# A linear-attention and MLP-mixer kernel: fp32 loads on the hardware queue, work moved to GpSimd, one activation table set, and two PSUM banks for three

## The chip, the cores and the metric

The kernel runs on one core of a Trainium2 chip. The metric is device time in microseconds of one execution. A core has TensorE (PE), VectorE (DVE), ScalarE (ACT), GpSimd (POOL) and SyncE (SP), each of which works through its own queue in order, and 16 DMA engines that all of them feed.

## The reference

Four batches, eight heads, 768 steps, head size 48. First a gated linear attention with a state per head, then a mixer: a token MLP (768 to 256 to 768) and a channel MLP (384 to 1536 to 384), each added to its input.

```python
f = 1.0 / (1.0 + np.exp(-f_logit))
for t in range(S):
    state = f[:, :, t, :, None] * state + np.einsum('bhd,bhe->bhde', k[:, :, t], v[:, :, t])
    y[:, :, t] = np.einsum('bhd,bhde->bhe', q[:, :, t], state)
# x = y with the heads side by side: (4, 768, 384)
h = np.maximum(xt @ w_tok1, 0.0) @ w_tok2          # xt = x transposed
u = x + h.transpose(0, 2, 1)
out = u + np.maximum(u @ w_ch1, 0.0) @ w_ch2
```

## The kernel before, in words

A sequence is cut into six chunks of 128 steps. For a whole batch (for batch 0: chunk 0, then the other five together) `prep_gates_slices` makes the logarithm of the gate on ACT, exp then ln, and splits it into two bf16 parts, Lhi (ACT) and Llo (DVE).

For each chunk `attn_front` sums the gates along time on PE into ps_S, and their totals into ps_dg. `attn_chunk` then makes G and Gi (ACT, exp of minus and plus the sum), multiplies q by G and k by Gi (qh and kh, both on DVE, lines 177 and 178), transposes both with eight matmuls against an identity into the two banks ps_AT, copies these as bf16 to qkT (q half on ACT, line 185, k half on DVE, line 186), multiplies k by q per head into the same banks (line 191), masks the result (AmT, two DVE operations, lines 200 and 201), and multiplies it with v into ps_y, to which the carried state adds its part. ACT copies ps_y to x_nat (fp32) and x_bf (bf16). Five DVE operations carry the state on.

`moe_slices` is the mixer of one batch: token matmuls (lines 247 and 254, evicted to h1T, u_nat and u_bf), transposes of u (line 268, to uT), 24 groups of three channel matmuls (line 280, each evicted to zT by ACT, one in three by DVE), and six groups of twelve output matmuls (line 298), added to u on DVE and stored by SP from two buffers out_sb. Its matmuls go round three PSUM banks. The mixer's six slices of one batch are written into the six chunks of the next batch's attention; a scheduler then puts the instructions of each engine in a fixed order, which the engine follows.

Loads: q, k and v are cast from fp32 to bf16 by DMAs that GpSimd issues; f_logit comes in fp32 on SP's queue. For batch 0 they are issued chunk by chunk, for the others in one DMA each. The weights are loaded, also cast, by GpSimd, after the inputs of batches 0 and 1. Batch b + 2 is loaded into the buffers of batch b. [...]

Of the kernel before, what the change touches and what calls it, by code (L numbers as in the profile page):

```python
# [17 lines left out]
def kernel(  # L18
# [24 lines left out]
    def st(shape, dtype, tag):  # L43
        return sb.tile(shape, dtype, tag=tag, name=tag)
# [19 lines left out]
        nc.gpsimd.dma_start(out=w_ch1, in_=moe_w_ch1.rearrange("(kt p) n -> p kt n", p=128))  # L64
        nc.gpsimd.dma_start(out=w_ch2, in_=moe_w_ch2.rearrange("(kt p) n -> p kt n", p=128))

    q_sb = [st([128, H, NCH, D], BF16, f"q_sb{i}") for i in range(2)]
    k_sb = [st([128, H, NCH, D], BF16, f"k_sb{i}") for i in range(2)]
    v_sb = [st([128, H, NCH, D], BF16, f"v_sb{i}") for i in range(2)]
    f_sb = [st([128, H, NCH, D], FP32, f"f_sb{i}") for i in range(2)]  # L70
    Lhi = [st([128, NCH, H, 64], BF16, f"Lhi{i}") for i in range(2)]
    Llo = [st([128, NCH, H, 64], BF16, f"Llo{i}") for i in range(2)]

    def load_batch_inputs(b, c0=0, c1=NCH):
        i = b % 2
        if (c0, c1) == (0, NCH):
            nc.gpsimd.dma_start(out=q_sb[i], in_=q[b].rearrange("h (c t) d -> t h c d", t=C))
            nc.gpsimd.dma_start(out=k_sb[i], in_=k[b].rearrange("h (c t) d -> t h c d", t=C))
            nc.gpsimd.dma_start(out=v_sb[i], in_=v[b].rearrange("h (c t) d -> t h c d", t=C))
            nc.sync.dma_start(out=f_sb[i], in_=f_logit[b].rearrange("h (c t) d -> t h c d", t=C))  # L80
            return
        for c in range(c0, c1):
            nc.sync.dma_start(out=f_sb[i][:, :, c, :],
                              in_=f_logit[b].rearrange("h (c t) d -> t h c d", t=C)[:, :, c, :])
            nc.gpsimd.dma_start(out=q_sb[i][:, :, c, :],
                                in_=q[b].rearrange("h (c t) d -> t h c d", t=C)[:, :, c, :])
            nc.gpsimd.dma_start(out=k_sb[i][:, :, c, :],
                                in_=k[b].rearrange("h (c t) d -> t h c d", t=C)[:, :, c, :])
            nc.gpsimd.dma_start(out=v_sb[i][:, :, c, :],
                                in_=v[b].rearrange("h (c t) d -> t h c d", t=C)[:, :, c, :])  # L90

    G = [st([128, H, 64], BF16, f"G{i}") for i in range(2)]
    Gi = [st([128, H, 64], BF16, f"Gi{i}") for i in range(2)]
# [17 lines left out]
    nc.vector.memset(state_bd, 0.0)  # L111

    ps_S = pt([128, 512], FP32, "ps_S")
    ps_AT = [pt([128, 4, 128], FP32, f"ps_AT{p}") for p in range(2)]
    ps_y = pt([128, H, D], FP32, "ps_y")
    ps_dg = pt([128, HP, 2 * D + 1], FP32, "ps_dg")
# [4 lines left out]
    uT = st([128, 3, S], BF16, "uT")  # L121
    zT = st([128, 12, S], BF16, "zT")
    out_sb = [st([128, DM], FP32, f"out_sb{i}") for i in range(2)]
    ps_moe = [pt([128, 512], FP32, f"ps_moe{i}") for i in range(3)]
    ring = [0]

    def moe_bank():
        ring[0] += 1
        return ps_moe[ring[0] % 3]

    def prep_gates_slices(b, c0=0, c1=NCH):
        ib = b % 2
# [33 lines left out]
    def attn_chunk(b, c, mid=(), front_next=None):  # L166
        i = c % 2
        ib = b % 2
        last = c == NCH - 1

        sview = ps_S.rearrange("t (h dd) -> t h dd", dd=64)[:, :, 0:D]
        nc.scalar.activation(G[i][:, :, 0:D], sview, AF.Exp, bias=0.0, scale=-1.0)
        nc.scalar.activation(Gi[i][:, :, 0:D], sview, AF.Exp, bias=0.0, scale=1.0)
        if not last:
            nc.scalar.activation(glast, ps_dg[:, :, 2 * D], AF.Exp, bias=0.0, scale=-1.0)  # L175

        nc.vector.tensor_tensor(qh[i][:, :, 0:D], q_sb[ib][:, :, c, :], G[i][:, :, 0:D], ALU.mult)
        nc.vector.tensor_tensor(kh[i][:, :, 0:D], k_sb[ib][:, :, c, :], Gi[i][:, :, 0:D], ALU.mult)

        qb, kb = blk(qh[i]), blk(kh[i])  # L180
        for hp in range(HP):
            nc.tensor.matmul(ps_AT[0][:, hp, :], lhsT=qb[:, hp, :], rhs=ident, start=True, stop=True)
        for hp in range(HP):
            nc.tensor.matmul(ps_AT[1][:, hp, :], lhsT=kb[:, hp, :], rhs=ident, start=True, stop=True)
        nc.scalar.copy(qkT[i][:, 0:4, :], ps_AT[0])  # L185
        nc.vector.tensor_copy(qkT[i][:, 4:8, :], ps_AT[1])  # L186

        for h in range(H):
            hp, par = h // 2, h % 2
            rows = slice(par * 64, par * 64 + D)  # L190
            nc.tensor.matmul(ps_AT[par][:, hp, :], lhsT=qkT[i][rows, 4 + hp, :],  # L191
                             rhs=qkT[i][rows, hp, :], start=True, stop=True)

        if front_next is not None:
            front_next()
        for m in mid:
            m()

        tb4 = tri_bf.unsqueeze(1).broadcast_to((128, 4, 128))
        nc.vector.tensor_tensor(AmT[i][:, 0:4, :], ps_AT[0], tb4, ALU.mult)  # L200
        nc.vector.tensor_tensor(AmT[i][:, 4:8, :], ps_AT[1], tb4, ALU.mult)

        for h in range(H):
            nc.tensor.matmul(ps_y[:, h, :], lhsT=AmT[i][:, (h % 2) * 4 + h // 2, :],
                             rhs=v_sb[ib][:, h, c, :],
                             start=(h == 0), stop=(c == 0 and h == H - 1),
                             skip_group_check=True)
        if c > 0:
            for hp in range(HP):
                nc.tensor.matmul(ps_y[:, 2 * hp:2 * hp + 2, :], lhsT=qkT[i][:, hp, :],  # L210
                                 rhs=state_bd[:, hp, :],
                                 start=False, stop=(hp == HP - 1), skip_group_check=True)
        if not last:
            for hp in range(HP):
                nc.tensor.matmul(ps_dg[:, hp, 0:2 * D], lhsT=kb[:, hp, :],
                                 rhs=v_sb[ib][:, 2 * hp:2 * hp + 2, c, :],
                                 start=True, stop=True)

        yflat = ps_y.rearrange("t h e -> t (h e)")
        nc.scalar.activation(x_nat[ib][:, c, :], yflat, AF.Copy, bias=0.0, scale=1.0)  # L220
        nc.scalar.activation(x_bf[ib][:, c, :], yflat, AF.Copy, bias=0.0, scale=1.0)

        if not last:
            nc.vector.tensor_tensor(state[0:D], state[0:D], ps_dg[0:D, :, 0:D], ALU.add)  # L224
            nc.vector.tensor_tensor(state[64:64 + D], state[64:64 + D],  # L225
                                    ps_dg[64:64 + D, :, D:2 * D], ALU.add)
            nc.vector.tensor_tensor(state, state, glast.unsqueeze(2).broadcast_to((128, HP, D)),  # L227
                                    ALU.mult)
            nc.vector.tensor_copy(state_bd[0:D, :, 0:D], state[0:D])
            nc.vector.tensor_copy(state_bd[64:64 + D, :, D:2 * D], state[64:64 + D])  # L230
# [7 lines left out]
    def moe_slices(b):  # L238
# [3 lines left out]

        def s_tok():
            for rt in range(2):
                pm = moe_bank()
                for kt in range(NCH):
                    nc.tensor.matmul(pm[:, 0:DM], lhsT=w_tok1[:, kt, rt * 128:(rt + 1) * 128],  # L247
                                     rhs=x_bf[ib][:, kt, :],
                                     start=(kt == 0), stop=(kt == NCH - 1))
                nc.scalar.activation(h1T[:, rt, :], pm[:, 0:DM], AF.Relu, bias=0.0, scale=1.0)  # L250
            for stt in range(NCH):
                pm = moe_bank()
                for kt in range(2):
                    nc.tensor.matmul(pm[:, 0:DM], lhsT=w_tok2[:, kt, stt * 128:(stt + 1) * 128],
                                     rhs=h1T[:, kt, :], start=(kt == 0), stop=(kt == 1))
                nc.vector.tensor_tensor(u_nat[:, stt, :], x_nat[ib][:, stt, :], pm[:, 0:DM], ALU.add)  # L256
                nc.scalar.activation(u_bf[:, stt, :], u_nat[:, stt, :], AF.Copy,  # L257
                                     bias=0.0, scale=1.0)
            if _DBG:
                nc.sync.dma_start(out=dbg_u[b].rearrange("(c t) n -> t c n", t=C), in_=u_nat)  # L260
                nc.sync.dma_start(out=dbg_h1[b], in_=h1T)
        sl.append(s_tok)

        def s_ut():
            for dmb in range(3):
                pm = moe_bank().bitcast(BF16)
                for stt in range(NCH):
                    nc.tensor.transpose(pm[:, stt * 128:(stt + 1) * 128],
                                        u_bf[:, stt, dmb * 128:(dmb + 1) * 128], ident)
# [5 lines left out]
        def s_ch(cc0, cc1, alt):  # L275
            for cc in range(cc0, cc1):
                for th in range(2):
                    pm = moe_bank()
                    for kt in range(3):
                        nc.tensor.matmul(pm[:, 0:384], lhsT=w_ch1[:, kt, cc * 128:(cc + 1) * 128],  # L280
                                         rhs=uT[:, kt, th * 384:(th + 1) * 384],
# [10 lines left out]
        def s_out():  # L292
            if _DBG:
                nc.sync.dma_start(out=dbg_zT[b], in_=zT)
            for tt in range(NCH):
                pm = moe_bank()
                for kt in range(12):
                    nc.tensor.matmul(pm[:, 0:DM], lhsT=zT[:, kt, tt * 128:(tt + 1) * 128],  # L298
                                     rhs=w_ch2[:, kt, :], start=(kt == 0), stop=(kt == 11))
# [6 lines left out]
    if _DBG:  # L306
# [2 lines left out]
        dbg_h1 = nc.dram_tensor("dbg_h1", (B, 128, 2, DM), BF16, kind="Internal").ap()  # L309
        dbg_uT = nc.dram_tensor("dbg_uT", (B, 128, 3, S), BF16, kind="Internal").ap()  # L310
        dbg_zT = nc.dram_tensor("dbg_zT", (B, 128, 12, S), BF16, kind="Internal").ap()
    load_batch_inputs(0, 0, 2)
    load_batch_inputs(0, 2, NCH)
    load_batch_inputs(1)
    load_weights()
    prev_moe: list = []
    for g in prep_gates_slices(0, 0, 1) + prep_gates_slices(0, 1, NCH):
        g()
    for b in range(B):
        ib = b % 2  # L320
        attn_batch_begin(b)
# [17 lines left out]
            nc.sync.dma_start(out=dbg_x[b].rearrange("(c t) n -> t c n", t=C),  # L339
                              in_=x_nat[b % 2])  # L340
        if b + 2 < B:
            load_batch_inputs(b + 2)
        prev_moe = moe_slices(b)
    for s in prev_moe:
        s()
# [30 lines left out]
```

## Time and profile before

| | us |
|---|---|
| median of 2 runs (242.51 to 243.28) | 242.89 |
| the profiled execution, its own time | 242.51 |
| its span, first to last instruction | 240.4 |

| engine | busy us | share of the span | instructions |
|---|---|---|---|
| PE, matmuls | 183.6 | 76% | 1673 |
| PE, weight loads | 111.5 | 46% | 1688 |
| DVE | 152.1 | 63% | 341 |
| ACT | 137.2 | 57% | 262 |
| POOL | 40.1 | 17% | 39 |

The software queue (GpSimd) moved 10.23 MB in 77168 packets, the hardware queue (SP) 9.44 MB in 14352.

How to read it: busy time is the sum over an engine's instructions. The profile also gives the span in 40 slices of 6 us, each digit the busy share of a slice in tenths. Groups show line, engine, operation and tile, with their count, sum, the mean of one in ns, and what ended the idle time before them. A view of waits says who waited for whom, with the total, the count and the longest. A view of stages gives each engine's busy time between two times, and a timeline gives start and duration of each instruction.

### The profile page before, as it was taken

The numbers are of one execution on the slowest core, as the hardware profiler recorded it, in microseconds if no ns is written. First come the engines' busy times: TensorE is split into PE (matmuls) and PEld (weight loads), VectorE is DVE, ScalarE is ACT, GpSimd is POOL, SyncE is SP. The second block draws the span as 40 slices with busy tenths as digits, with TensorE's granted clock in tenths as the row PEclk, the third lists the DMA queues.
The fourth block names the chain that finished last, engine by engine and source line by source line (L and its number), as shares of the span: only waits on it lengthen the run. The fifth ranks groups of instructions, "written<-read, shape, count | busy, mean of one in ns | idle before, by whom it ended". The sixth has DMA issues, their size and how long they took to land.

```text
span 240.4 us, 4273 instructions
## 1 busy us (share of the span) xinstructions
PE 183.6 (76%) x1673; PEld 111.5 (46%) x1688; DVE 152.1 (63%) x341; ACT 137.2 (57%) x262; POOL 40.1 (17%) x39
## 2 busy tenths in 40 slices
PE   0413376103858999999999999999999999989993
PEld 0201253001535555566565555666556556546661
DVE  4323769300965999995489998637999872444221
ACT  5479999900697765870376777008776710556300
POOL 9823910821302100150300000000000000000000
PEclk9999999999965999999999999999999999999999
DMA  8999999999999900099490000121000002100022
GB/s 113 147 185 151 163 158 137 174 144 198 208 182 137 103 3 0 3 85 174 135 104 0 3 1 3 65 100 35 0 3 0 3 33 102 64 0 0 8 107 85
DMA packets 91539, 19.93 MB, mean 83 GB/s; under 512 B 80896, under 2 KB 91136, under 8 KB 91520
## 3 DMA queue, kind: packets, MB, share of 16 engines
q0 software_dynamic: 77168, 10.23, 78.3%
q1 hardware_dynamic: 14352, 9.44, 18.4%
q8 instruction: 13, 0.21, 0.4%
q14 instruction: 6, 0.05, 0.1%
HBM read 25.17 MB, written 4.72 MB: 124 GB/s over the span
## 4 chain that ended last, share of the span: by engine, by line
PE 34%; DVE 26%; DMA 15%; issue 9%; ACT 8%; POOL 7%; DVEq 0%; POOLq 0%
DMA q_sb_77<-in_q_dram 6%; DMA w_tok_73<-in_moe_w_tok_dram 6%; PE ps_moe_135 L298 5%; PE ps_moe_133 L298 5%; PE ps_moe_134 L298 5%; PE ps_moe_133 L280 3%; DMA out_dram<-out_sb_132 3%; DVE zT L285 3%; PE ps_moe_134 L280 3%; PE ps_moe_135 L280 3%; DVE u_nat L256 2%; DVE qkT_98 L186 2%; DVE AmT_99 L200 2%; DVE uT L270 2%; DVE state L225 2%
## 5 line engine op out<-in xcount | busy, mean ns | idle before, releaser
L298 PEld LDWEIGHTS <-zT 128*128 128x128 bf16 x288 | 27.7, 98 | 18.3
L280 PEld LDWEIGHTS <-w_ch_75 128*128 128x128 bf16 x288 | 26.5, 97 | 19.9 <-issue 4.5
L280 PE MATMUL ps_moe_133<-uT,w_ch_75 128*128 128x384 bf16 x96 | 22.9, 325 | 1.4 <-DVE uT L270 0.5
L280 PE MATMUL ps_moe_135<-uT,w_ch_75 128*128 128x384 bf16 x96 | 22.6, 325 | 0.8 <-DVE zT L285 0.5
L280 PE MATMUL ps_moe_134<-uT,w_ch_75 128*128 128x384 bf16 x96 | 22.2, 325 | 0.5 <-DVE zT L285 0.3
L220 ACT ACTIVATE x_nat_105<-ps_y 128x384 f32<-128x384 f32 x12 | 6.0, 499 | 24.8 <-PE ps_y L210 24.2
L298 PE MATMUL ps_moe_134<-w_ch_76,zT 128*128 128x384 bf16 x96 | 17.3, 326 | 0.0
L200 DVE TENSOR_TENSOR AmT_100<-ps_AT_122,tri_bf 128x512 bf16<-128x512 f32 x12 | 8.3, 688 | 14.2 <-PE ps_AT_123 L191 14.0
L298 PE MATMUL ps_moe_135<-w_ch_76,zT 128*128 128x384 bf16 x96 | 17.1, 326 | 0.0
L298 PE MATMUL ps_moe_133<-w_ch_76,zT 128*128 128x384 bf16 x96 | 17.1, 326 | 0.0
L287 ACT ACTIVATE zT<-ps_moe_134 128x384 bf16<-128x384 f32 x22 | 10.9, 496 | 8.0 <-PE ps_moe_134 L280 7.8
L161 PE MATMUL ps_dg<-ones_bf,Lhi_85 128*128 128x1 bf16 x40 | 3.5, 166 | 13.5 <-ACT Lhi_85 L143 6.7
L287 ACT ACTIVATE zT<-ps_moe_135 128x384 bf16<-128x384 f32 x22 | 11.0, 500 | 4.9 <-PE ps_moe_135 L280 4.8
L220 ACT ACTIVATE x_nat_104<-ps_y 128x384 f32<-128x384 f32 x12 | 5.8, 486 | 13.9 <-PE ps_y L210 13.9
L247 PE MATMUL ps_moe_134<-x_bf_106,w_tok_73 128*128 128x384 bf16 x6 | 2.5, 452 | 14.1 <-DMA w_tok_73<-in_moe_w_tok_dram 12.2
L247 PEld LDWEIGHTS <-w_tok_73 128*128 128x128 bf16 x48 | 4.6, 105 | 17.9 <-DMA w_tok_73<-in_moe_w_tok_dram 12.4
L287 ACT ACTIVATE zT<-ps_moe_133 128x384 bf16<-128x384 f32 x20 | 10.0, 500 | 4.3 <-PE ps_moe_133 L280 4.2
L224 DVE TENSOR_TENSOR state<-state,ps_dg 48x192 f32<-48x192 f32 x20 | 6.8, 342 | 8.5 <-ACT qkT_98 L185 4.9
L257 ACT ACTIVATE u_bf<-u_nat 128x384 bf16<-128x384 f32 x24 | 11.0, 519 | 1.8 <-DVE u_nat L256 1.6
L200 DVE TENSOR_TENSOR AmT_99<-ps_AT_122,tri_bf 128x512 bf16<-128x512 f32 x12 | 8.2, 685 | 6.0 <-PE ps_AT_123 L191 5.7
L175 ACT ACTIVATE glast<-ps_dg 128x4 f32<-128x4 f32 x20 | 3.6, 178 | 14.1 <-DVE state L227 12.7
L191 PE MATMUL ps_AT_122<-qkT_97 48*128 48x128 bf16 x48 | 5.1, 232 | 7.3 <-ACT qkT_97 L185 5.5
(149 smaller groups left out, 470.3 us busy)
## 6 DMA issues: line engine op xcount, KB each, us to landing
out_dram<-out_sb_131 SPq DMA_DIRECT2D x12, 192.0 KB, 1.9
out_dram<-out_sb_132 SPq DMA_DIRECT2D x12, 192.0 KB, 1.9
f_sb_83<-in_f_logit_dram SPq DMA_DIRECT2D x6, 192.0 KB, 5.7
q_sb_78<-in_q_dram POOLq DMA_DIRECT2D x2, 576.0 KB, 12.6
k_sb_80<-in_k_dram POOLq DMA_DIRECT2D x2, 576.0 KB, 18.2
v_sb_82<-in_v_dram POOLq DMA_DIRECT2D x2, 576.0 KB, 11.6
w_ch_75<-in_moe_w_ch_dram POOLq DMA_DIRECT2D x1, 1152.0 KB, 20.3
w_ch_76<-in_moe_w_ch_dram POOLq DMA_DIRECT2D x1, 1152.0 KB, 24.9
```

What stands on the lines that cost most here:

```text
L186: nc.vector.tensor_copy(qkT[i][:, 4:8, :], ps_AT[1])
L191: nc.tensor.matmul(ps_AT[par][:, hp, :], lhsT=qkT[i][rows, 4 + hp, :], rhs=qkT[i][rows, hp, :], start=True, stop=True)
L200: nc.vector.tensor_tensor(AmT[i][:, 0:4, :], ps_AT[0], tb4, ALU.mult)
L220: nc.scalar.activation(x_nat[ib][:, c, :], yflat, AF.Copy, bias=0.0, scale=1.0)
L224: nc.vector.tensor_tensor(state[0:D], state[0:D], ps_dg[0:D, :, 0:D], ALU.add)
L225: nc.vector.tensor_tensor(state[64:64 + D], state[64:64 + D], ps_dg[64:64 + D, :, D:2 * D], ALU.add)
L247: nc.tensor.matmul(pm[:, 0:DM], lhsT=w_tok1[:, kt, rt * 128:(rt + 1) * 128], rhs=x_bf[ib][:, kt, :], start=(kt == 0), stop=(kt == NCH - 1))
L257: nc.scalar.activation(u_bf[:, stt, :], u_nat[:, stt, :], AF.Copy, bias=0.0, scale=1.0)
L280: nc.tensor.matmul(pm[:, 0:384], lhsT=w_ch1[:, kt, cc * 128:(cc + 1) * 128], rhs=uT[:, kt, th * 384:(th + 1) * 384], start=(kt == 0), stop ...
L285: nc.vector.tensor_scalar(dst, pm[:, 0:384], 0.0, None, ALU.max)
L287: nc.scalar.activation(dst, pm[:, 0:384], AF.Relu, bias=0.0, scale=1.0)
L298: nc.tensor.matmul(pm[:, 0:DM], lhsT=zT[:, kt, tt * 128:(tt + 1) * 128], rhs=w_ch2[:, kt, :], start=(kt == 0), stop=(kt == 11))
```

## The change

q, k and v are loaded in fp32 by SP's hardware queue, with f_logit, chunk by chunk for every batch. v goes through a single fp32 buffer v_ld and is cast to bf16 by GpSimd, one chunk at a time. k is gated on GpSimd instead of DVE, from fp32; q is still gated on DVE, from fp32. The transposes of q and k become transposes with a bf16 result, taken in turn (q, k, q, k, ...), into a bank of their own (ps_tr), and one DVE copy takes all eight to qkT. For that bank the mixer gives up one of three. The weights are issued after batch 0's inputs and ahead of batch 1's. The gates of batch 0 are prepared chunk by chunk. A table set that holds both exp and ln is loaded once at the start.

```diff
-    q_sb = [st([128, H, NCH, D], BF16, f"q_sb{i}") for i in range(2)]
-    k_sb = [st([128, H, NCH, D], BF16, f"k_sb{i}") for i in range(2)]
+    q_sb = [st([128, H, NCH, D], FP32, f"q_sb{i}") for i in range(2)]
+    k_sb = [st([128, H, NCH, D], FP32, f"k_sb{i}") for i in range(2)]
+    v_ld = [st([128, H, NCH, D], FP32, "v_ld")] * 2
...
-    def load_batch_inputs(b, c0=0, c1=NCH):
+    def load_batch_inputs(b, step):
         i = b % 2
...
+        for c in range(0, NCH, step):
+            for dst, src in ((f_sb, f_logit), (q_sb, q), (k_sb, k), (v_ld, v)):
+                nc.sync.dma_start(out=dst[i][:, :, c:c + step, :],
+                                  in_=src[b].rearrange("h (c t) d -> t h c d", t=C)[:, :, c:c + step, :])
+            nc.gpsimd.tensor_copy(v_sb[i][:, :, c:c + step, :], v_ld[i][:, :, c:c + step, :])
...
+    ps_tr = pt([128, 8, 128], BF16, "ps_tr")
...
-    ps_moe = [pt([128, 512], FP32, f"ps_moe{i}") for i in range(3)]
+    ps_moe = [pt([128, 512], FP32, f"ps_moe{i}") for i in range(2)]
...
-        nc.vector.tensor_tensor(kh[i][:, :, 0:D], k_sb[ib][:, :, c, :], Gi[i][:, :, 0:D], ALU.mult)
+        nc.gpsimd.tensor_tensor(kh[i][:, :, 0:D], k_sb[ib][:, :, c, :], Gi[i][:, :, 0:D], ALU.mult)
...
         for hp in range(HP):
-            nc.tensor.matmul(ps_AT[0][:, hp, :], lhsT=qb[:, hp, :], rhs=ident, start=True, stop=True)
-        for hp in range(HP):
-            nc.tensor.matmul(ps_AT[1][:, hp, :], lhsT=kb[:, hp, :], rhs=ident, start=True, stop=True)
-        nc.scalar.copy(qkT[i][:, 0:4, :], ps_AT[0])
-        nc.vector.tensor_copy(qkT[i][:, 4:8, :], ps_AT[1])
+            nc.tensor.transpose(ps_tr[:, hp, :], qb[:, hp, :], ident)
+            nc.tensor.transpose(ps_tr[:, 4 + hp, :], kb[:, hp, :], ident)
+        nc.vector.tensor_copy(qkT[i], ps_tr)
...
-                    pm = moe_bank()
+                    pm = ps_moe[th]
...
-    load_batch_inputs(0, 0, 2)
-    load_batch_inputs(0, 2, NCH)
-    load_batch_inputs(1)
+    nc.scalar.preload_act_table_set("natural_log_exp_and_others")
+    load_batch_inputs(0, 1)
     load_weights()
+    load_batch_inputs(1, 1)
     prev_moe: list = []
-    for g in prep_gates_slices(0, 0, 1) + prep_gates_slices(0, 1, NCH):
-        g()
+    for c in range(NCH):
+        for g in prep_gates_slices(0, c, c + 1):
+            g()
```

More of the change, by code (lines that the diff above doesn't have):

```diff
@@ L72 @@
     Llo = [st([128, NCH, H, 64], BF16, f"Llo{i}") for i in range(2)]
-    def load_batch_inputs(b, c0=0, c1=NCH):
+    def load_batch_inputs(b, step):
         i = b % 2
[L76 to L90, printed above, removed]
+        for c in range(0, NCH, step):
[3 more added lines that the diff above has]
+            nc.gpsimd.tensor_copy(v_sb[i][:, :, c:c + step, :], v_ld[i][:, :, c:c + step, :])
     G = [st([128, H, 64], BF16, f"G{i}") for i in range(2)]
@@ L123 @@
     out_sb = [st([128, DM], FP32, f"out_sb{i}") for i in range(2)]
-    ps_moe = [pt([128, 512], FP32, f"ps_moe{i}") for i in range(3)]
[L125 to L129, printed above, removed]
+    ps_moe = [pt([128, 512], FP32, f"ps_moe{i}") for i in range(2)]
     def prep_gates_slices(b, c0=0, c1=NCH):
@@ L244, in s_tok @@
             for rt in range(2):
-                pm = moe_bank()
+                pm = ps_moe[rt]
                 for kt in range(NCH):
@@ L251, in s_tok @@
             for stt in range(NCH):
-                pm = moe_bank()
+                pm = ps_moe[stt % 2]
                 for kt in range(2):
@@ L265, in s_ut @@
             for dmb in range(3):
-                pm = moe_bank().bitcast(BF16)
+                pm = ps_moe[dmb % 2].bitcast(BF16)
                 for stt in range(NCH):
@@ L277, in s_ch @@
                 for th in range(2):
-                    pm = moe_bank()
+                    pm = ps_moe[th]
                     for kt in range(3):
@@ L295, in s_out @@
             for tt in range(NCH):
-                pm = moe_bank()
+                pm = ps_moe[tt % 2]
                 for kt in range(12):
@@ L341 @@
         if b + 2 < B:
-            load_batch_inputs(b + 2)
+            load_batch_inputs(b + 2, 1)
         prev_moe = moe_slices(b)
```

## The prediction

> **What bounds the kernel now.** I read the page's slices first, then the trace cut into stages, the waits, the DMA queues, and the timeline where a number was needed. The slices show two regimes. Up to slice 12 (72 us) DMA is full and PE mostly idle; from slice 14 to the end PE is full.
>
> ```profile
> span 240.4 us, 4273 instructions
> PE   0413376103858999999999999999999999989993
> DVE  4323769300965999995489998637999872444221
> DMA  8999999999999900099490000121000002100022
> ```
>
> The stage marks are the first h1T eviction (L250) of each batch, 77.97, 120.94, 164.62 and 206.54 us: from there that batch's MLP runs on PE. The first cut, at 58.2, is where PE wakes from its longest wait.
>
> ```profile
> core 0: us, PE busy (x) PEld busy (x) DVE busy (x) ACT busy (x) POOL busy (x), PEclk, DMA share, GB/s
> 0.00:58.20 58.20, 16.34 (x155) 10.09 (x158) 24.67 (x56) 40.52 (x47) 29.07 (x34) 1.00 2.33 155
> 58.20:77.97 19.77, 15.01 (x128) 9.12 (x130) 13.87 (x30) 14.24 (x24) 3.62 (x2) 0.74 1.87 180
> 77.97:120.94 42.97, 41.09 (x414) 25.10 (x417) 36.00 (x79) 23.91 (x56) 7.44 (x4) 1.00 0.92 71
> 120.94:164.62 43.68, 42.08 (x419) 25.96 (x423) 33.88 (x82) 24.52 (x59) 0.00 (x0) 1.00 0.34 42
> 164.62:206.54 41.92, 40.30 (x386) 24.66 (x388) 31.78 (x74) 22.32 (x53) 0.00 (x0) 1.00 0.07 27
> 206.54:240.40 33.86, 28.77 (x179) 16.58 (x177) 11.93 (x23) 11.65 (x24) 0.00 (x0) 1.00 0.11 39
> ```
>
> The reader is to see that each of the three middle stages (MLP of one batch beside attention of the next) keeps PE 96% busy, so an edit there gains almost nothing and loses whenever it makes PE wait. ACT, at 24 of 43 us, has slack. The 78 us of start are where time can be won: there PE waits for w_tok.
>
> ```profile
> PE ps_moe_134 L247 <- DMA w_tok_73<-in_moe_w_tok_dram: 12.2, 1, 12.2
> ```
>
> **What the Trainium skill says.** DMA: Bandwidth & Descriptors, "Queues, rings and completion order", says that each DMA engine takes turns between its queues packet by packet. The trace agrees: in the window 15 to 18 us both queues moved equally many packets, though one packet held 8 times the bytes.
>
> ```profile
> DMA packets 1240, 0.54 MB, mean 178 GB/s; under 512 B 620, under 2 KB 1240, under 8 KB 1240
> q1 hardware_dynamic: 620, 0.48, 103.8%
> q0 software_dynamic: 620, 0.06, 37.5%
> ```
>
> SBUF — State Buffer, "Who interferes with whom", says that a VectorE instruction in a two-port mode, or with two SBUF inputs, and a GpSimd instruction block each other for a whole instruction. The trace has such a case: a state_bd cast beside a GpSimd DMA issue took 2.06 us, its neighbour of the same form 0.26.
>
> ```profile
> 26.11 2.24 POOL L77 DMA_DIRECT2D q_sb_78<-in_q_dram  x1
> 26.37 2.06 DVE L229 CAST state_bd<-state 48x192 bf16<-48x192 f32 x1
> 28.46 0.26 DVE L230 CAST state_bd<-state 48x192 bf16<-48x192 f32 x1
> ```
>
> ScalarE: Activation LUTs, "Table sets: the hidden batching unit", says that one set holds both exp and ln; the trace here shows 11 table loads of 1283 ns, the last at 71.97 us, so they cost only in the start.
>
> **The change part by part.** I use the build order of the changed kernel (what stands behind what on each queue) with durations from this trace.
>
> 1. *Start, gain.* In the new order POOL holds: cast of v chunk 0, issue of w_tok1, w_tok2, w_ch1, cast of chunk 1, issue of w_ch2, cast of chunk 2, and only then the first k gating. So attention of batch 0 can't begin before v of chunk 2 has landed. When is that? The hardware queue starts at 1.9 us and, alone, moved 192 B packets at about 250 GB/s (window 0 to 3 us), 1.3 per ns; a chunk of f, q, k, v is 4 x 1024 packets, about 3.2 us. v of chunk 0 lands near 6, its cast (0.5) ends at 6.6, and weights flow about 2 us after their issue (first q issue 1.64, first packet 3.75), from 8.9 us. By then 8750 packets have moved. The weights are 2944 packets and took 53.9 to 71.0 us less a little other traffic, so 16 us; with packet turns only 2944 of ours pass beside them (2.3 us more). They end at 27.2; v of chunk 2, packet 12288, follows at 27.7 and is seen at 28.6.
>  DVE then has Llo of chunk 3 ahead of its first qkT copy: f of chunk 3 seen 29.6, three ACT passes of 0.52, Llo 0.56 gives 31.8. From there DVE carries per chunk: Llo 0.56, qh 0.56 (now fp32 in, so priced as the 128x384 fp32 Llo row, not as the 0.355 of today), qkT 0.69, two AmT 1.3, five state operations 1.57, together 4.7 us; with small gaps 5.3. Five more chunks end at 58.3; AT, AmT, y, x_bf and w_tok1 matmuls add 4.5: h1T at 63 instead of 78.0. **Gain 15 us.** All weights are there by then, so the 12.2 us wait goes. The table loads go too and are inside this number: ACT isn't what is late in the new start.
>
> 2. *Stage 1, loss.* In the old PE order batch 1's attention is woven into batch 0's channel matmuls. In the new one, 18 of 24 channel groups stand before batch 1's first gate sum has even finished, five chunks follow with almost no channel work between them, and the output matmuls come behind the last chunk's AT. So: h1T to first channel matmul 6.1 us (206.54 to 212.62 in the last stage) plus 1.5 (item 3); 18 groups at 0.63 = 11.3; ACT runs the three 2.1 us gate passes between evictions, and with two banks PE waits about 1.5 for each, 4.5. Attention starts 23.5 us after h1T. First chunk to its qkT 2.6, five more at 4.6 (DVE 4.1 without Llo, and gaps) 23, AT 0.5; then 67 output matmuls 10.9, plus 2 because SP now issues loads of batch 3 between the stores; last y, x_bf and token matmuls 2. Sum 64.5 instead of 43. **Loss 21.5.** The inputs don't hold it: batch 1's load ends near 58, before 63.
>
> 3. *Two MLP banks for three.* In the last stage, three banks and nothing beside it:
>
> ```profile
> 214.54 0.65 PE L280 MATMUL ps_moe_133<-uT,w_ch_75 128*128 128x384 bf16 x3
> 215.23 0.49 ACT L287 ACTIVATE zT<-ps_moe_133 128x384 bf16<-128x384 f32 x1 [0.15 <-PE ps_moe_133 L280]
> ```
>
>  A group issues in 0.49 us, but its bank is taken for 0.65 + 0.04 + 0.49 (ACT; DVE 0.56) + 0.05 = 1.23 to 1.30. Three banks allow a group each 0.42, so PE sets the pace; two allow one each 0.63. 24 groups lose 0.14 each, 3.4 us; token groups (bank 1.13, two banks 0.57 against 0.46) 0.6; the third uT block waits for the first copy, 0.9. **Last stage +4.9.** Output groups (1.95 us each) lose nothing. In stages 2 and 3 attention fills part of this: between 0 and 4.9, I take 2 each.
>
> 4. *k gating and v cast on POOL.* The GPSIMD Engine Reference, "Elementwise — side-by-side cycle accounting", gives 4497 ns for 2048 elements; an estimate for 384 is 0.84 us, against 0.35 on DVE; the cast I put between 0.32 and 0.84, at 0.5. POOL's total, 24 x 1.34 = 32 us, hides. DVE loses 0.35 and gains 0.2 per chunk, but qh, the state product and two casts may stand behind POOL: 1.34 of 5 us, so up to 27% of 4 operations by 0.4 us each, 0.4 us per chunk. Net +0.25, about 1.5 us per stage; from -1 (PE hides it) to +5.
>
> 5. *Transposes and one qkT copy.* Same count on PE. A 1024-element bf16 copy out of PSUM lies between the 768 row (0.55) and that row scaled (0.73): 0.69, what DVE pays today; ACT is freed of 0.6 per chunk. A bank apart from ps_AT lets transposes run before AmT is done. Worth up to 2 us per stage where the chain is late, nothing where PE is full; I take -1.5.
>
> Stages 2 and 3 each: +2 +1.5 -1.5 = +2.
>
> Sum on the profiled span: 240.4 - 15 + 21.5 + 2 + 2 + 4.9 = 255.8. The execution took 242.5, 2.1 more than its span, and the median is 0.4 above that: 258.
>
> **The rivals.**
> - *Weights don't starve the loads* (ends within 2%). If the queues shared by bytes, our queue would keep about 110 GB/s beside the weights: the remaining 3540 packets to v of chunk 2 (0.68 MB) need 6.2 us, landing at 15. All of the start moves by 13 us, until chunk 5's own arrival near 38 decides: 258 - 13 = 245. Against it stand the equal packet counts. It wins if the first k gating runs before 20 us.
> - *The overlap in stage 1 survives* (faster). If batch 1's attention took the slots left by two banks and channel work filled its chain as today, stage 1 would stay near 43: 258 - 21.5 = 236.5. For it: DVE has only 36 of 43 us there today. Against: PE runs its queue in order.
> - *POOL and VectorE block each other far more* (slower still): k gating at 1.5 us instead of 0.84 and every blocked operation waiting for it whole adds about 0.5 us to each of 24 chunks: 258 + 12 = 270.
>
> **How the numbers follow.** Forecast 258: chance 0.52; sharing by bytes 245: 0.18; overlap survives 236.5: 0.13; port blocking 270: 0.17. The unknowns of the forecast (stage 1 by 5, stages 2 and 3 by 3 each, the start by 4) make about 250 to 266 for itself. The range for 8 in 10 takes in part of both neighbours: 240 to 271. A measurement of this kernel tells about 2% from no change (238.0 to 247.7 is the same): faster 0.14 (the overlap case and a little of the sharing case), same 0.18, slower 0.68.
>
> **What would show it.** Right: first k gating near 29 us behind the third v cast; h1T of batch 0 near 63, of batch 1 near 128; PE with gaps in both halves of stage 1; channel groups 0.63 us apart in the last stage, which lasts about 38.7; one table load. Wrong: h1T of batch 1 before 112 us (the overlap survived), chunk loads that arrive evenly beside the weights, or a last stage near 34.

## The result, and the profile after

The changed kernel takes 257.42 us (median of two runs, 256.96 and 257.89) against 242.89: a ratio of 1.060, with a 95% interval of 1.049 to 1.071. It is slower. The forecast was 258 us, and the profiled span is 256.1 us where the working gave 255.8. The sum holds, but the term of the start held because two errors in it cancelled, which is luck, and the runs below correct some of the reasons given.

The slices of the changed kernel, to be read against those of before: PE is at work earlier, then isn't full for long before slice 17, and DMA is busy to slice 15 (slices are counted from 0; one is 6.4 us). The PEclk row is the granted clock of PE in tenths.

```profile
span 256.1 us, 4360 instructions
PE   0300168676795885899988989999799999789994
DVE  4200059894631499976699998438998842542231
PEclk9999999976897798589999999999999999999999
DMA  7999999999999998019999000121000012000022
```

The trace cut at the same marks, the first h1T eviction (now L235) of each batch:

```profile
core 0: us, PE busy (x) PEld busy (x) DVE busy (x) ACT busy (x) POOL busy (x), PEclk, DMA share, GB/s
0.00:60.68 60.68, 23.74 (x247) 14.75 (x249) 28.06 (x73) 21.10 (x48) 14.81 (x27) 0.96 1.11 180
60.68:126.59 65.91, 54.66 (x452) 30.96 (x454) 41.97 (x81) 35.91 (x65) 12.54 (x19) 0.83 0.89 149
126.59:174.30 47.71, 43.58 (x421) 26.52 (x423) 37.37 (x77) 26.58 (x56) 8.14 (x11) 1.00 0.43 80
174.30:217.89 43.59, 41.02 (x386) 25.23 (x388) 31.88 (x69) 19.70 (x49) 4.00 (x5) 1.00 0.07 26
217.89:256.10 38.21, 31.31 (x179) 16.43 (x177) 12.42 (x23) 11.81 (x24) 0.00 (x0) 1.00 0.10 34
```

| us | start | stage 1 | stage 2 | stage 3 | last |
|---|---|---|---|---|---|
| before | 78.0 | 43.0 | 43.7 | 41.9 | 33.9 |
| after | 60.7 | 65.9 | 47.7 | 43.6 | 38.2 |
| difference | -17.3 | +22.9 | +4.0 | +1.7 | +4.3 |
| predicted | -15 | +21.5 | +2 | +2 | +4.9 |

Stage 1 decides the sign: without it the change would have gained 7 us. Its PE clock (0.83) says that PE had stretches with too little to do: in the stretches 60.7 to 86.7 and 86.7 to 112.0 us the granted clock was 0.77 and 0.80. The Trainium skill, TensorE: Matmul & The Clock Gate, "What's actually happening", says that an idle PE falls back to half its clock. From slice 8 on the trace agrees: the PEclk row shows 0.5 to 0.9 in slices 8 to 17, and 0.9 or more once PE is full. A channel matmul of 128x384 took 0.52 us from 100 to 110 us, where the granted clock was 0.51, and 0.32 from 130 to 170. So a PE that waits pays twice, since its next matmuls run slowly. The first slices of the row can't be read that way: it shows 0.9 there, though PE was mostly idle and a gate sum of 128x512 took about 0.60 us, against 0.38 from 130 us on.

Where the first k gating stands, on GpSimd's timeline:

```profile
14.10 0.50 POOL L81 CAST v_sb_82<-v_ld 128x384 bf16<-128x384 f32 x1 [4.25 <-DMA v_ld<-in_v_dram]
14.54 1.03 POOL L65 DMA_DIRECT2D w_ch_76<-in_moe_w_ch_dram  x1
32.14 0.51 POOL L81 CAST v_sb_82<-v_ld 128x384 bf16<-128x384 f32 x1 [16.57 <-DMA v_ld<-in_v_dram]
32.61 0.91 POOL L165 TENSOR_TENSOR kh_96<-k_sb_79,Gi_92 128x384 bf16<-128x384 f32 x1
```

The third v chunk is waited for 16.6 us, and k of chunk 0 stands behind its cast. Why v is that late is seen in the DMA view of the window 15 to 18 us, the same window as in the prediction:

```profile
q0 software_dynamic: 228, 0.59, 99.3%
q1 hardware_dynamic: 227, 0.04, 12.8%
```

The columns are packets, MB, and time as a share of the span. One packet each, whatever its size: 228 of the weights and 227 of the load. This is the turn-taking that the Trainium skill describes in DMA: Bandwidth & Descriptors, "Queues, rings and completion order". Before, the hardware queue moved 620 packets of 768 B (0.48 MB) in this window against 620 small ones. Now its packets are the small ones, 192 B, and those of the weights the large ones: it got 0.04 MB. The weights took from 9.8 to 30.2 us, and in that time the load got 4081 packets against their 3008.

In the last stage a channel group comes every 0.63 us (228.58 to 231.11 is four of them), not every 0.49:

```profile
228.58 0.65 PE L265 MATMUL ps_moe_136<-uT,w_ch_75 128*128 128x384 bf16 x3
229.32 0.65 PE L265 MATMUL ps_moe_135<-uT,w_ch_75 128*128 128x384 bf16 x3
229.88 0.65 PE L265 MATMUL ps_moe_136<-uT,w_ch_75 128*128 128x384 bf16 x3
230.62 0.65 PE L265 MATMUL ps_moe_135<-uT,w_ch_75 128*128 128x384 bf16 x3
231.11 0.65 PE L265 MATMUL ps_moe_136<-uT,w_ch_75 128*128 128x384 bf16 x3
```

### The profile page after: what moved, and what is told of

Its sections match the earlier page's. It is cut to its first block, busy times and chain, and to the rows that moved or that the text cites. A ratio compares the mean times of both kernels' runs of the same rounds, so it can differ in the third digit from the quotient of the medians.

```text
span 256.1 us, 4360 instructions
## 1 busy us (share of the span) xinstructions
PE 194.3 (76%) x1678; PEld 113.9 (44%) x1688; DVE 151.7 (59%) x321; ACT 115.1 (45%) x240; POOL 39.5 (15%) x60
## 3 DMA queue, kind: packets, MB, share of 16 engines
q0 software_dynamic: 3008, 3.15, 7.2%
## 5 line engine op out<-in xcount | busy, mean ns | idle before, releaser
L265 PEld LDWEIGHTS <-w_ch_75 128*128 128x128 bf16 x288 | 27.9, 100 | 31.5 <-issue 17.9
L283 PEld LDWEIGHTS <-zT 128*128 128x128 bf16 x288 | 27.7, 98 | 18.3 <-issue 0.3
L133 DVE TENSOR_TENSOR Llo_88<-f_sb_84,Lhi_86 128x384 bf16<-128x384 f32 (+1 forms) x7 | 5.9, 841 | 25.4 <-ACT Lhi_86 L130 25.4
L270 DVE TENSOR_SCALAR zT<-ps_moe_136 128x384 bf16<-128x384 f32 x16 | 8.9, 554 | 12.9 <-PE ps_moe_136 L265 12.9
L286 DVE TENSOR_TENSOR out_sb_134<-u_nat,ps_moe_136 128x384 f32<-128x384 f32 x12 | 6.6, 553 | 15.6 <-PE ps_moe_136 L283 13.6
L141 PE MATMUL ps_S<-Lhi_86,tri_bf 128*128 128x512 bf16 x10 | 4.6, 461 | 14.4 <-ACT Lhi_86 L130 13.8
L124 ACT ACTIVATE f_sb_84<-f_sb_84 128x384 f32<-128x384 f32 (+1 forms) x7 | 5.2, 749 | 21.1 <-DMA f_sb_84<-in_f_logit_dram 21.1
L286 DVE TENSOR_TENSOR out_sb_133<-u_nat,ps_moe_135 128x384 f32<-128x384 f32 x12 | 6.6, 554 | 13.4 <-PE ps_moe_135 L283 13.4
L242 ACT ACTIVATE u_bf<-u_nat 128x384 bf16<-128x384 f32 x24 | 12.0, 522 | 4.3 <-DVE u_nat L241 3.8
L170 PE MATMUL ps_tr<-ident,kh_96 128*128 128x128 bf16 x48 | 8.1, 242 | 7.6 <-POOL kh_96 L165 7.6
L81 POOL CAST v_sb_82<-v_ld 128x384 bf16<-128x384 f32 x12 | 6.4, 536 | 29.6 <-DMA v_ld<-in_v_dram 29.6
L165 POOL TENSOR_TENSOR kh_97<-k_sb_80,Gi_93 128x384 bf16<-128x384 f32 x6 | 5.5, 909 | 35.5 <-ACT Gi_93 L160 28.8
L270 DVE TENSOR_SCALAR zT<-ps_moe_135 128x384 bf16<-128x384 f32 x16 | 8.9, 554 | 2.6 <-PE ps_moe_135 L265 2.4
```

Of the source, the lines that this page charges most:

```text
L81: nc.gpsimd.tensor_copy(v_sb[i][:, :, c:c + step, :], v_ld[i][:, :, c:c + step, :])
L124: nc.scalar.activation(fb, fb, AF.Exp, bias=0.0, scale=-1.0)
L133: nc.vector.tensor_tensor(Llo[ib][:, c0:c1, :, 0:D], fbc, Lhi[ib][:, c0:c1, :, 0:D], ALU.subtract)
L165: nc.gpsimd.tensor_tensor(kh[i][:, :, 0:D], k_sb[ib][:, :, c, :], Gi[i][:, :, 0:D], ALU.mult)
L170: nc.tensor.transpose(ps_tr[:, 4 + hp, :], kb[:, hp, :], ident)
L270: nc.vector.tensor_scalar(dst, pm[:, 0:384], 0.0, None, ALU.max)
```

## The experiments

Theory: stage 1 lost its overlap through the order of the program, the start was set by packets and by GpSimd's queue, and two banks cost some 9 us in all. Rivals: the landing of batch 1 holds stage 1; GpSimd and VectorE block each other. All runs, with medians, ratios to the kernel before on the same chip, and the stages of the profiled run:

| kernel | us | ratio (95%) | start | 1 | 2 | 3 | last |
|---|---|---|---|---|---|---|---|
| 1 changed, batches 1 to 3 loaded whole | 255.29 | 1.050 (1.047 to 1.053) | 61.5 | 61.4 | 48.0 | 43.6 | 38.4 |
| 2 changed, k gated on VectorE | 257.24 | 1.057 (1.054 to 1.061) | 57.7 | 66.8 | 48.3 | 43.9 | 38.2 |
| 3 changed, three banks | 248.64 | 1.021 (1.018 to 1.025) | 65.0 | 56.8 | 49.0 | 43.3 | 33.4 |
| 4 before, two banks | 253.19 | 1.041 (1.037 to 1.046) | 78.2 | 47.7 | 44.7 | 43.0 | 38.4 |
| 5 before, weights ahead of batch 1 | 239.67 | 0.987 (0.985 to 0.990) | 74.0 | 44.3 | 43.7 | 41.9 | 33.9 |
| 6 as 5, one table load | 239.49 | 0.986 (0.984 to 0.989) | 72.8 | 45.0 | 43.7 | 41.9 | 33.9 |
| 7 changed, no channel weights loaded | 245.09 | 1.009 (1.007 to 1.012) | 48.2 | 66.0 | 47.7 | 43.6 | 38.2 |
| 8 as 3, with 1 and 2 | 239.96 | 0.989 (0.987 to 0.992) | 61.1 | 54.8 | 45.9 | 42.7 | 33.7 |
| 9 as 8, channel weights held back | 232.55 | 0.959 (0.954 to 0.963) | 50.9 | 57.1 | 45.6 | 42.7 | 33.7 |
| 10 as 9, only f loaded whole | 234.63 | 0.966 (0.963 to 0.968) | 51.3 | 58.2 | 45.1 | 42.7 | 33.8 |
| 11 as 8, k gated on GpSimd | 248.48 | 1.026 (1.022 to 1.030) | 70.2 | 50.0 | 48.4 | 43.3 | 33.8 |
| 12 as 8, all loads by chunks | 248.53 | 1.021 (1.019 to 1.024) | 58.6 | 64.3 | 47.7 | 42.7 | 33.4 |

### Loads of batches 1 to 3 whole

```diff
-    load_batch_inputs(1, 1)
+    load_batch_inputs(1, NCH)
...
-            load_batch_inputs(b + 2, 1)
+            load_batch_inputs(b + 2, NCH)
```

> The changed kernel with batches 1 to 3 loaded as whole tensors (f, then q, k, v; 4 transfers a batch for 24), same queue, same bytes. Batch 0 stays chunk by chunk. The whole of f of batch 1 then lands near 51 us instead of 69, ahead of q, k and v, and the build puts batch 1's gate sums among the token matmuls and its chunks among the channel matmuls. Theory (stage 1 lost its overlap because batch 1's gates come late in the program's order, behind f of the last chunk): start unchanged near 60.7 us, stage 1 back from 65.9 to 43 to 50, total 235 to 243. Rival 1 (the load itself, 4.7 MB a batch in 192 B packets, holds stage 1; v of batch 1 now lands whole at 69 or later, so not earlier): stage 1 stays at 60 or more, total 252 to 260. Rival 2 (two banks and POOL hold stage 1): stage 1 near 60, total 250 to 254.

The packets of a whole load turned out to be 768 B, not 192 B as written there. Stage 1 came down only to 61.4, and the total to 255.3, the numbers of rival 1. In this run batch 2's first chunks also moved ahead of the second mark, so the third mark is the fair one: 170.9 us, 3.4 ahead of the changed kernel. The order alone, with two banks and k on GpSimd, does not give the stage back. Runs 8 and 12 below speak against rival 1's reason.

This run shows GpSimd and VectorE blocking each other. A whole v is cast in one instruction, and VectorE's state product beside it took 2.25 us; the same operation, another time, 0.36:

```profile
99.11 2.43 POOL L81 CAST v_sb<-v_ld 128x2304 bf16<-128x2304 f32 x1
```

```profile
99.51 2.25 DVE L212 TENSOR_TENSOR state<-state,glast 128x192 f32<-128x192 f32 x1
```

### k gated on VectorE

```diff
-        nc.gpsimd.tensor_tensor(kh[i][:, :, 0:D], k_sb[ib][:, :, c, :], Gi[i][:, :, 0:D], ALU.mult)
+        nc.vector.tensor_tensor(kh[i][:, :, 0:D], k_sb[ib][:, :, c, :], Gi[i][:, :, 0:D], ALU.mult)
```

> The changed kernel with k gated on VectorE, as in the kernel before; v is still cast on GpSimd. Theory (POOL's order held the start: the first k gating stood behind the cast of v chunk 2, at 32.6 us): first k gating near 12 us, first h1T near 51 instead of 60.7, limited then by chunk 5's own arrival near 45; stage 1 can't follow by as much, because f of batch 1 lands near 69 as before; total 240 to 250. Rival 1 (packets set the start, not POOL's order): first h1T stays at 58 to 61, total 254 to 258. Rival 2 (GpSimd and VectorE block each other on their port): stages 2 and 3 fall by 2 or more each, from 47.7 and 43.6; the theory gives them 0 to 1 each.

The first k gating moved from 32.6 to 10.3 us, and the mark only from 60.7 to 57.7. So GpSimd's order was not what set the start: the chunks were still landing (the cast of chunk 5 began at 45.5 us). Little of the 3 us reached the end: PE's order now has 69 of 72 channel matmuls ahead of the first of batch 1's gate sums (45 in the changed kernel), and stages 1 to 3 grew by 1.7 together. Rival 2 fails too, with two banks: with GpSimd free of k, stages 2 and 3 did not fall.

### Three banks in the changed kernel, two in the kernel before

Run 3 puts the ring of three and the transposes of before into the changed kernel; run 4 is one number in the kernel before:

```diff
-    ps_moe = [pt([128, 512], FP32, f"ps_moe{i}") for i in range(3)]
+    ps_moe = [pt([128, 512], FP32, f"ps_moe{i}") for i in range(2)]
...
-        return ps_moe[ring[0] % 3]
+        return ps_moe[ring[0] % 2]
```

> The changed kernel with three MLP banks in rotation and, to make room, q and k transposed as before (plain matmuls into the two AT banks, two copies on ACT and VectorE). Loads, weights, cast and k gating as changed. Theory (two banks cost 4.4 in the last stage and some 2 in each stage before it): last stage from 38.2 to 33.9 to 34.5, channel groups 0.49 us apart, stages 2 and 3 down by 2 each, start unchanged, total 247 to 251. Rival (banks are covered by attention where there is any): only the last stage falls, total 252 to 254. Rival (last stage is slowed by something else, stores or clock): last stage stays at 38, total 256 to 258.

> The kernel before with two MLP banks in rotation instead of three and nothing else changed. Theory: last stage from 33.9 to 38.3, stages 1 to 3 up by 1 to 2 each, total 249 to 254. Rival (attention fills the waits): last stage alone, total 247 to 248. Rival (the pace of the last stage is not the banks'): 242 to 244.

The last stage of each, run 3 and then run 4:

```profile
214.15:247.60 33.45, 28.76 (x179) 16.57 (x177) 11.94 (x23) 11.65 (x24) 0.00 (x0) 0.98 0.11 40
```

```profile
213.61:252.00 38.39, 30.89 (x179) 16.44 (x177) 12.47 (x23) 11.84 (x24) 0.00 (x0) 0.99 0.10 34
```

Same work, 4.9 us apart, and 33.9 and 38.2 in the kernels they come from: the last stage's loss is the bank's, both ways. In the kernel before two banks cost 10 us by the medians, 11.6 on the spans: 4.5 in the last stage, 1.1 and 1.0 in stages 3 and 2, 4.7 in stage 1. In the changed kernel the third bank, with the transposes of before, gives 8.5 of the span back (256.1 to 247.6). Stage 1 fell by 9.1 and the start grew by 4.3, where none was expected. Stages 2 and 3, expected to fall by 2 each, went from 47.7 to 49.0 and from 43.6 to 43.3. In stage 2 PE's granted clock was 0.52 from 147 to 154 us; why it did not fall is open.

### The kernel before with its weights early

```diff
-    load_batch_inputs(1)
     load_weights()
+    load_batch_inputs(1)
```

Run 6 has one line more, ahead of all loads:

```diff
+    nc.scalar.preload_act_table_set("natural_log_exp_and_others")
```

> The kernel before with one edit: the four weight loads are issued ahead of batch 1's loads, on the same GpSimd queue. All else as before (three banks, cast loads, k gated on VectorE, 11 table loads). Theory 1 (what has to be moved before stage 1 can run, two batches and the weights, ends at 71 us whatever the order, so a start won by moving the weights is given back in stage 1 while batch 1 is still landing): first h1T near 60 to 66 instead of 78, q, k, v of batch 1 landing to 71, stage 1 from 43 to 48 to 56, total 232 to 240. Theory 2 (the long stage 1 of the changed kernel is its own: its order, banks and GpSimd work): start 60 to 66, stage 1 stays at 43 to 45, total 225 to 231.

> The run with the weights early in the kernel before, and also the table set that holds exp and ln loaded once at the start (one table load for 11). Theory (table loads sit on ACT in the start, where the loads decide): 0 to 3 us less than the same kernel without it. Rival (ACT's 13 us of table loads are late work of the start once the weights no longer are): 5 to 10 us less, first h1T at 55 or below.

Neither theory's start came: 74.0, not 60 to 66. PE's order has gate sums and other attention work of batch 1 among the token matmuls, ahead of the mark, so that the mark can't come before batch 1's inputs: just ahead of it, at 71.1 us, PE ends a wait of 2.7 us for v. The gain is 1.3%. The one table load adds nothing that can be told from it (0.987 and 0.986), though ACT was busy 13 us less in the start. The changed kernel's own swap of these two lines does nothing at all: there the inputs are on the other queue, and with the two calls swapped back the build gives every engine the same instructions in the same order.

### No channel weights

```diff
-        nc.gpsimd.dma_start(out=w_ch1, in_=moe_w_ch1.rearrange("(kt p) n -> p kt n", p=128))
-        nc.gpsimd.dma_start(out=w_ch2, in_=moe_w_ch2.rearrange("(kt p) n -> p kt n", p=128))
+        nc.vector.memset(w_ch1, 0.01)
+        nc.vector.memset(w_ch2, 0.01)
```

> The changed kernel without the loads of the two channel weights (2.3 MB): they are filled with a constant by VectorE at the start instead. w_tok is loaded as before, and PE's order in stage 1 is the same. Theory (packets of the weights take turns with those of the load and hold the load back; w_ch packets have 2304 of some 3000): second to last chunks of batch 0 land 10 to 13 us earlier, first k gating near 19 us instead of 32.6, first h1T near 49, and stage 1 unchanged within 3, total 243 to 248. Rival (queues don't hold each other, bytes or the order of GpSimd's queue do): first k gating at 28 or later, first h1T at 57 or later, total 253 or more.

The first k gating came at 19.3 us, the mark at 48.2, the total at 245.1; expected were 19, 49 and 243 to 248:

```profile
18.39 0.98 POOL L81 CAST v_sb<-v_ld 128x384 bf16<-128x384 f32 x1 [4.68 <-DMA v_ld<-in_v_dram]
19.33 0.91 POOL L165 TENSOR_TENSOR kh<-k_sb,Gi 128x384 bf16<-128x384 f32 x1
```

The channel weights' packets cost the changed kernel 12.5 us of start. They are 1952 of the software queue's 3008 packets (1056 are left here), not the 2304 written there. Stage 1 takes 66.0 us against 65.9. This alone doesn't tell the order of the program from the landing of batch 1, since the landing moved with the mark: the cast of the sixth and last v chunk begins 10.7 us after the mark here and 10.8 us after it in the changed kernel.

The trace of the changed kernel does tell them apart. The last packet of batch 1's f starts at 66.5 us. The first gate pass on that f (line 124) starts at 75.02, straight behind an eviction on ACT, with no idle time before it. Batch 1's attention begins only at 86.65 us (its first G), over 14 us after the last cast of batch 1 had ended:

```profile
71.53 0.51 POOL L81 CAST v_sb_83<-v_ld 128x384 bf16<-128x384 f32 x1 [4.22 <-DMA v_ld<-in_v_dram]
74.64 0.49 ACT L272 ACTIVATE zT<-ps_moe_135 128x384 bf16<-128x384 f32 x1 [0.25 <-PE ps_moe_135 L265]
75.02 2.12 ACT L124 ACTIVATE f_sb_85<-f_sb_85 128x2304 f32<-128x2304 f32 x1
```

In this stage neither PE, ACT nor VectorE waits for a load of batch 1. With the order as it was built, the order holds the stage, not the landing.

### Three banks with whole loads, with VectorE, and with both

Run 8 has both; runs 11 and 12 each take one away.

The edits are those of runs 1, 2 and 3:

```diff
-    load_batch_inputs(1, 1)
+    load_batch_inputs(1, NCH)
...
-        nc.gpsimd.tensor_tensor(kh[i][:, :, 0:D], k_sb[ib][:, :, c, :], Gi[i][:, :, 0:D], ALU.mult)
+        nc.vector.tensor_tensor(kh[i][:, :, 0:D], k_sb[ib][:, :, c, :], Gi[i][:, :, 0:D], ALU.mult)
...
-    ps_moe = [pt([128, 512], FP32, f"ps_moe{i}") for i in range(2)]
+    ps_moe = [pt([128, 512], FP32, f"ps_moe{i}") for i in range(3)]
```

> The changed kernel's loads and nothing else of its compute: q, k, v in fp32 on the hardware queue (batch 0 by chunks, later batches whole), v cast on GpSimd, weights ahead, one table set; but k gated on VectorE, three MLP banks and the transposes of the kernel before. Theory 1 (landing of batch 1 and the order that follows from it hold stage 1, beside the banks): start near 58 to 61, stage 1 at 50 to 57, last stage 33.5, total 238 to 246. Theory 2 (stage 1 was long for the banks and for GpSimd's gating): stage 1 at 43 to 46, total 225 to 233.

> The run with whole loads, three banks and k gated on VectorE, with the k gating put back on GpSimd, as the change has it. Theory (gating k on GpSimd costs little by itself: 0.91 against 0.56 us in the chain of a chunk, and now and then a blocked VectorE operation): 1 to 4 us more than with VectorE, in the start and stage 1; stages 2 and 3 within 1. Rival (blocking on the port, or POOL's order, is a large part of what the change lost): 6 to 12 us more.

> The changed kernel with three banks (transposes as before) and k gated on VectorE, all loads by chunks as the change has them. It differs from the run at 240.0 only in the loads of batches 1 to 3, and from the run at 248.6 only in who gates k. In this order all 72 channel matmuls of batch 0 and 23 of its output matmuls stand ahead of batch 1's first gate sum. Theory (the order decides: f of batch 1 by chunks comes last, so the build puts its attention behind the channel matmuls, and neither the banks nor the gating alone mends that): start 57 to 58, stage 1 at 60 or more, total 247 to 252. Rival (k gating on GpSimd was what was left of the loss beside the banks): stage 1 at 55 or less, total 239 to 243.

With three banks: neither 248.6, whole loads alone 248.5, VectorE alone 248.5, both 240.0. Each edit is worth nothing without the other, and together some 8 us (these runs were taken on four chips, on which the kernel before took 242.4 to 243.2). In run 12 VectorE shortens the start by 6.4, but PE then has all 72 channel matmuls and 23 output matmuls ahead of batch 1's first gate sum, and stage 1 gives back 7.4. In run 11 the order is woven, with batch 1's gate sum inside the token matmuls, but batch 0 begins late because k waits behind the third cast (the first k gating at 32.3 us, 10.1 in run 8). The first 30 us of runs 11 and 8:

```profile
0.00:30.00 30.00, 4.39 (x26) 1.65 (x26) 5.86 (x21) 8.78 (x17) 5.46 (x14) 1.00 1.13 181
```

```profile
0.00:30.00 30.00, 9.62 (x85) 5.41 (x86) 12.76 (x36) 10.44 (x22) 5.41 (x14) 1.00 1.15 183
```

Five us of PE work and seven of VectorE are done before 30 us in run 8 and after it in run 11. This part is the cost of k's place in GpSimd's queue. It isn't all that run 11 loses: of 7.5 us of span between it and run 8, 4.4 are there at the second mark, 2.5 more come in stage 2 and 0.6 in stage 3. Blocking may be a part of the 2.5: in stage 2 of run 11 three casts of the state beside GpSimd's work took 0.55, 2.15 and 0.97 us in place of 0.26. The two causes weren't separated.

Runs 8 and 12 differ only in the loads of batches 1 to 3. The last cast of batch 1's v began at 70.5 us in run 8 and at 71.9 in run 12, and still the third mark stands at 161.8 us in run 8 and at 170.5 in run 12. So it isn't when the whole of batch 1 has landed that decides. f came earlier in run 8 (its last packet starts at 50.0 us), and through it the order changed: batch 1's first gate sum stands ahead of all channel matmuls. A part of the difference can be the clock, which was 0.83 in stage 1 of run 12 and 0.96 in that of run 8; no run separates it from the order, since a PE that waits more also gets the lower clock.

The theory's numbers for runs 8 and 12 were met, but for starts up to 0.6 us later. For run 11 the rival's were (6 to 12 us more), and the theory's limit of 1 us for stage 2 was missed. How the loss of stage 1 divides between order and banks to the microsecond stays open, since the build's order changes with the banks too.

### Channel weights held back

```diff
+        for w in (w_ch1, w_ch2):
+            nc.gpsimd.tensor_copy(w[:, 0, 0:1], v_sb[0][:, 0, NCH - 1, 0:1])
         nc.gpsimd.dma_start(out=w_ch1, in_=moe_w_ch1.rearrange("(kt p) n -> p kt n", p=128))
```

> The run with whole loads from batch 1, k gated on VectorE and three banks, and with the two channel weights held back: each gets one element written by GpSimd from the last cast v of batch 0, so that its load can't be issued before. PE's order is the same. Theory (channel weights' packets hold batch 0 back and aren't needed before the first channel matmul): first h1T from 61 to near 48 and, with f and q of batch 1 at 4 elements (768 B) a packet, little delay of these; stage 1 grows by 3 to 8 since v of batch 1 still lands near 69; total 229 to 235. Rival (what lands by 70 us decides, whatever the order): the start's gain goes into stage 1 whole, total 237 to 240. Rival (slower): the channel weights now land after the first channel matmul wants them, 240 to 244.

> As the run with the channel weights held back, but of batches 1 to 3 only f is loaded whole, ahead, and q, k, v by chunks (192 B packets). Theory (attention of batch 1 can then run chunk by chunk as it lands, instead of waiting for all of v): stage 1 shorter than in that run by 2 to 6, total 227 to 233. Rival (192 B packets lose the turns against the weights, so chunks land late): equal or up to 5 slower.

One element written from the last cast makes the loads wait for it. They are issued at 33.7 us, behind batch 0:

```profile
32.67 0.51 POOL L83 CAST v_sb<-v_ld 128x384 bf16<-128x384 f32 x1 [3.76 <-DMA v_ld<-in_v_dram]
33.24 0.31 POOL L65 COPY w_ch<-v_sb 128x1 bf16<-128x1 bf16 x2
33.73 0.76 POOL L66 DMA_DIRECT2D w_ch<-in_moe_w_ch_dram  x1 [0.18 <-POOL w_ch L65]
```

The start falls by 10.2, to 50.9 (48 was expected), stage 1 gives 2.3 back, and 232.55 us beats both kernels (0.959 of before). Chunked q, k, v of the later batches, in run 10, are no better than whole: 234.6, which the rival expected.

## Why the prediction was right or wrong

- **Start.** The gain was right (17.3 for 15), but two terms of it were off and cancelled. The weights were to take 18.3 us beside the load, ending at 27.2; they took 20.4 and ended at 30.2. So the first k gating came at 32.6 instead of near 29. Against this, a chunk took 4.05 us in the start (six qkT copies from 35.35 to 55.61), not 5.3. The rate of the hardware queue alone was also too high: 1.3 packets per ns, from its first 3 us, where sustained it moves 0.93 (13948 in the 15 us from 40 to 55). So batch 1's last cast began at 71.5, where its load was to end near 58. And too much of the start was put down to GpSimd's order: run 2 gives that 3 us, run 7 gives the weights' packets 12.5.
- **Stage 1.** 22.9 for 21.5, and from the order that the working read: attention began 26.0 us after the mark (23.5 predicted), its six qkT copies took 21.4 us (89.17 to 110.57; 23 predicted), the three gate passes cost PE 3.1 us of waits (4.5), and the output matmuls stood behind. The step "the inputs don't hold it: batch 1's load ends near 58" was wrong in its number and right in its conclusion, as the trace of the changed kernel shows. The working has no term for the clock, which was 0.83 in this stage; what it cost isn't known. What the working did not see either is that no one edit undoes this loss.
- **Two banks.** 4.3 in the last stage for 4.9; runs 3 and 4 measure 4.8 and 4.5. Stages 2 and 3 pay 1.0 and 1.1 for it (run 4) where 2 was taken.
- **GpSimd.** k gating took 0.91 to 1.05 us (estimate 0.84), a cast 0.51 (0.5). The blocking was real but small in the changed kernel: the state product rose from a mean of 353 ns to 439 over 20 instructions, 1.7 us in all. Run 2 shows no gain in stages 2 and 3 when k goes back, so the +1.5 per stage was too much. k's place in GpSimd's queue cost more, 3 us of the start in run 2, and there stage 1 took it back. With three banks and whole loads gating k on GpSimd cost 8.5 us (runs 11 and 8), from its place in the queue and perhaps from blocking.
- **Transposes and one copy.** The copy took 0.69 as priced. Runs 3, 8 and 12 undo this part together with the banks, so the 1.5 us per stage credited to it was not measured by itself and stays open.
- **Rivals.** Sharing by bytes falls with 228 packets to 227. The overlap did not survive: the second mark was at 126.6. Blocking on the port to 1.5 us per k gating did not appear.

## What to carry to other kernels

Before pricing a faster start, look at what the program's order puts behind it: work that can't be woven in because one input comes last turns a won start into a long next stage, and edits that each remove one of two such obstacles measure as nothing. In this kernel two queues shared the DMA engines by packets, so moving a load to small packets beside large ones hands the bandwidth away; hold back what isn't needed yet. Price a PSUM bank where matmuls stand alone: with two banks for three a channel group came every 0.63 us in place of 0.49.

## What the runs showed of the hardware that was not expected

In these runs packets of 192 B moved nearly as many bytes as those of 768 B as long as no other queue had work. With nothing beside it, the hardware queue was read from 40 to 55 us in the changed kernel (192 B packets) and from 45 to 60 in run 8 (768 B): 176 and 187 GB/s, the MB of these lines by 15 us:

```profile
q1 hardware_dynamic: 13948, 2.64, 115.2%
```

```profile
q1 hardware_dynamic: 3697, 2.81, 106.0%
```

The first line is the changed kernel's, the second that of run 8, which moved the bytes in about a quarter of the packets. So small packets cost 6% alone; beside the weights, at one packet each in turn, the load fell to 0.04 MB in 3 us, about 14 GB/s, mostly beside the weights' largest packets (3072 B), and to 38 GB/s over the 20.4 us of all the weights.
